# hv of six batches as seven half-size products over even and odd tokens, in a linear-attention and gated-MLP kernel

## The chip, the cores and the metric

The kernel runs on one NeuronCore of one Trainium2 chip. The metric is the device time of one execution in microseconds (us). Before the change it is 513.96 us, the median of two runs (513.74 and 514.18).

## The reference

Eight batches of 576 tokens go through two layers. The attention part has 8 heads of 64 and no softmax: k and v of a head make one 64x64 matrix, q is multiplied by it, and each head's 64 outputs are normalized by their root mean square. The result is `x`, 576 x 512 for a batch. The second part is a spatially gated MLP:

```
kv = einsum('bhsd,bhse->bhde', k, v);  out = einsum('bhsd,bhde->bhse', q, kv)
x  = out / sqrt(mean(out*out) + 1e-6) * g_norm          # heads side by side: 576 x 512
h  = maximum(x @ w_in, 0);  u, v = h[..., :512], h[..., 512:]
v_n = (v - mean(v)) / sqrt(var(v) + 1e-6)
v_s = einsum('ts,bsd->btd', w_spatial, v_n) + b_spatial[None, :, None]
y  = (u * v_s) @ w_out
```

So there are four large products in a batch. In the kernel's names they are hv (x by the V half of w_in), u (x by the U half), the spatial product (w_spatial by v_n) and out (gated by w_out).

## The kernel before, in words

**Number format.** Every large product is made of three TensorE matmuls in place of one. Both operands are split into a high part (a rounding copy on ScalarE, `split`, L325) and a low part (the difference, on VectorE, L326). `hl` lists the three pairs high-high, high-low and low-high. Names that end in H and L are these two parts: XH and XL of x, VH and VL of v_n, GH and GL of the gated product, WVH and WVL of w_in's V half, WUH and WUL of its U half, WSH and WSL of w_spatial.

**Tiles.** 576 tokens are four chunks of 128 and a tail of 64. The tails of two batches, an even and the odd one after it, are computed together in one 128-token chunk (`hv_tail`, and the out unit with the number NC). S is 576, NT 512, HS 288 (half the tokens), HF 256 (half of 512 features).

**The four products of a batch from 2 on.** hv (`hv`, L312) takes the four chunks one by one: 4 steps over the 512 rows of w_in, three pairs each, so 12 matmuls whose moving operand is 512 columns wide. The chunk's x is the stationary operand. `hv_end` then takes it out of PSUM with one ReLU on ScalarE, normalizes it and splits it. u and the spatial product are already made by Winograd's form of Strassen's scheme: seven half-size products p1 to p7 in place of eight (`u_steps` L481, `sp_steps` L574), each for two halves q of 128 rows. A product is 6 matmuls of 288 columns here. It needs sums of quarter blocks of both operands: those of x are made in each batch (`x_sums`, tiles T, L427), those of the V quarter blocks too (`sums`, L343), those of the weights once. p6, p7 and p4 add up in one PSUM bank (b), p5 and p3 in another (c), p1 and p2 in a third (a), and VectorE or ScalarE reads a bank between them. out (`out_unit`, L632) is 12 matmuls of 512 columns for each chunk.

**Buffers.** Four PSUM banks (`ps_mm`) serve all large products. SBUF is full, so two buffers take turns. One holds G (the gated product) during the spatial and out products and the sums T during u. The other holds w_out during out and three extra forms of w_in's U half (UX) during u. Both are refilled from DRAM copies (spare_u, spare_o) by DMAs on GpSimd's queue (`to_u` L861, `to_out` L871).

**Order.** The first two batches are issued from a table of tokens (PLAN, L35), since weights are decoded there from 64-bit numbers. From batch 2 on the loops at L916 to L976 issue, for batch b: `to_u`, `x_sums`, the hv chunks, the seven u products twice, the spatial products, the out chunks. Between them `step()` issues one piece of the attention of a later batch (k-v products `pskv`, q products `pso`, transposes `pstr`, normalizing). Within the limits of data and buffers a list scheduler then settles the order on each engine.

Attention loads go on SyncE's queue, the loads of UX and w_out on GpSimd's.

Of the kernel before, what the change touches and what calls it, by code (L numbers as in the profile page):

```python
# [47 lines left out]
def body(ctx: ExitStack, tc, qT, kvm, kvt, g2, w_in, wsT, bsp, w_out, out):  # L48
# [16 lines left out]
    WVH = persistent([P, NP, FH], F32R, "WVH")  # L65
    WVL = persistent([P, NP, FH], F32R, "WVL")
# [3 lines left out]
    spare_u = dram.tile([P, 2, 2, 3, HF], F32, name="spare_u", tag="spare_u")  # L70
# [5 lines left out]
    WSH = persistent([P, 2, 7, HS], F32R, "WSH")  # L76
    WSL = persistent([P, 2, 7, HS], F32R, "WSL")
# [21 lines left out]
    gcol = persistent([P, 16], F32, "gcol")[:, 0:1]  # L99
    edge = ctx.enter_context(tc.tile_pool(name="edge", bufs=1, side="right"))  # L100
# [216 lines left out]

    def hv_k(c, k, ps):
        cols = slice(c * P, (c + 1) * P)
        pairs = hl(XH[:, k, cols], XL[:, k, cols], WVH[:, k], WVL[:, k])  # L320
        for i, (lt, rh) in enumerate(pairs):
            nc.tensor.matmul(ps, lt, rh, start=k == 0 and i == 0, stop=k == NP - 1 and i == 2)  # L322
# [34 lines left out]
    def hv_tail():  # L357
# [3 lines left out]
                   hl(XH[:, k, cols], XL[:, k, cols], WVH[:, k], WVL[:, k])])  # L361
        v = work.tile([P, FH], F32, name="v", tag="v", bufs=3)
        layer_norm(ps, v, nc.vector)
        d = work.tile([P, HS], F32, name="d", tag="g")[:, 0:HF]
# [10 lines left out]
    def hv_32(c, k):  # L375
        nc.tensor.matmul(psv[c], X32[:, k, c * P:(c + 1) * P], W32[k], start=k == 0,
                         stop=k == NP - 1)

    def hv_tail_32():
# [7 lines left out]
        d = work.tile([P, HS], F32, name="d", tag="g")[:, 0:HF]  # L387
# [25 lines left out]
    def split_g():  # L413
        for d in range(4):
            split(GH[:, d], GL[:, d], U[:, d, 0:NT])
            split(GT[:, 0, d, 0:TAIL], GT[:, 1, d, 0:TAIL], U[:, d, NT:S])

    def u_unit(b, d, j):
# [5 lines left out]
                               XH[:, k, cols], XL[:, k, cols])])  # L424
# [7 lines left out]
    def x_sums_():  # L432
        for k in range(2):
            q = []
            for of, j, name in ((0, 0, "p1"), (2, 1, "u2"), (0, 1, "u3"), (2, 0, "g")):
                q.append(work.tile([P, HS], F32, name=name, tag=name))
                x = [f32(x[:, of + k, j * HS:(j + 1) * HS]) for x in (XH, XL)]
                nc.vector.tensor_tensor(q[-1], *x, op=ALU.add)
            q11, q22, q12, q21 = q
            nc.vector.tensor_tensor(q11, q12, q11, op=ALU.subtract)  # L440
            nc.vector.tensor_tensor(q12, q22, q12, op=ALU.subtract)
            nc.vector.tensor_tensor(q22, q22, q11, op=ALU.subtract)
            nc.vector.tensor_tensor(q21, q21, q22, op=ALU.subtract)
            for n, x in (1, q22), (0, q11), (2, q12), (3, q21):
                split(TH[n][:, k], TL[:, n, k], x)

    def w_sums(kk):
# [8 lines left out]
        for x, n in (first[:, HF:FH], slice(0, 1)), (second, slice(1, 3)):  # L456
# [3 lines left out]
            for i, w in enumerate(parts):  # L460
                nc.sync.dma_start(spare_u[:, i, kk, n], f32(w))

    def u_product(ps, q, n, of, start=True, stop=True):

        cols = slice(q * P, (q + 1) * P)
        raw = {0: (0, 0), 1: (2, 0), 2: (2, 1)}
        pairs = []
        for k in range(2):
            if n < 4:
                w = [x[:, k, n, cols] for x in (WUH, WUL)]  # L470
            else:
                w = [UX[:, i, k, n - 4, cols] for i in range(2)]
            if of in raw:
                at, j = raw[of]
                x = [x[:, at + k, j * HS:(j + 1) * HS] for x in (XH, XL)]
            else:
                x = [TH[of - 3][:, k], TL[:, of - 3, k]]
            pairs += hl(*w, *x)
        multiply(ps, pairs, start, stop)

    def u_steps():  # L481

        st = {}

        def bank(q, name):
            st[q, name] = ps_mm.tile([P, 512], F32, name=f"psu{name}", tag="mm")[:, 0:HS]
            return st[q, name]

        def temp(q, name):
            st[q, name] = work.tile([P, HS], F32, name=name, tag=name)  # L490
            return st[q, name]

        def own(q, i, j):
            return U[:, 2 * i + q, j * HS:(j + 1) * HS]

        def p1(q):
            ps = bank(q, "a")
            u_product(ps, q, 0, 0)
            nc.scalar.copy(temp(q, "p1"), ps)

        def p2(q):
            ps = st.pop((q, "a"))
            u_product(ps, q, 1, 1, False)
            nc.scalar.copy(own(q, 0, 0), ps)

        def p6(q):
            ps = bank(q, "b")
            u_product(ps, q, 3, 4)
            nc.vector.tensor_tensor(temp(q, "u2"), ps, st[q, "p1"], op=ALU.add)

        def p5(q):
            ps = bank(q, "c")
            u_product(ps, q, 6, 3)

        def p7(q):
            ps = st[q, "b"]
            u_product(ps, q, 4, 5, False)
            nc.vector.tensor_tensor(temp(q, "u3"), ps, st[q, "p1"], op=ALU.add)
            nc.vector.tensor_tensor(own(q, 1, 1), st[q, "c"], st.pop((q, "u3")), op=ALU.add)

        def p4(q):
            ps = st.pop((q, "b"))
            u_product(ps, q, 2, 6, False)
            nc.vector.tensor_tensor(own(q, 1, 0), ps, st.pop((q, "p1")), op=ALU.add)

        def p3(q):
            ps = st.pop((q, "c"))
            u_product(ps, q, 5, 2, False)
            nc.vector.tensor_tensor(own(q, 0, 1), ps, st.pop((q, "u2")), op=ALU.add)

        return [lambda f=f, q=q: f(q) for f, q in
                ((p1, 0), (p1, 1), (p2, 0), (p2, 1), (p6, 0), (p5, 0), (p7, 0), (p6, 1), (p4, 0), (p3, 0),
                 (p5, 1), (p7, 1), (p4, 1), (p3, 1))]

    def product(ps, q, n, of, start=True, stop=True):
# [4 lines left out]
                                                      WSH[:, k, of], WSL[:, k, of])], start, stop)  # L540
# [16 lines left out]
    def gate(b, d, j, ps, add=None):  # L557
# [3 lines left out]
        g = work.tile([P, HS], F32, name="g", tag="g")  # L561
# [4 lines left out]
        if j == 0:  # L566
            split(GH[:, d, cols], GL[:, d, cols], g)
# [453 lines left out]
```

## Time and profile before

| | |
|---|---|
| median of the runs shown | 513.96 us |
| the profiled execution | 512.66 us |
| its span, first to last instruction | 510.9 us |
| TensorE busy | 498.2 us (98%) |
| TensorE weight loads busy | 437.9 us (86%) |
| VectorE busy | 412.3 us (81%) |
| ScalarE busy | 291.0 us (57%) |
| GpSimd busy | 21.5 us (4%) |
| moved by DMA | 72.24 MB, 141 GB/s on average |
| mean granted TensorE clock | 0.996 |

The profiled execution takes 1.76 us more than its span, and the median is 1.30 us above it. "PE" is TensorE's matmuls, "PEld" its weight loads, which overlap the matmuls. A matmul's duration in the profile includes the depth of the array, so consecutive matmuls overlap in it; what one costs in a stream is the step from start to start, which is read from a run of matmuls and their count. DVE is VectorE, ACT ScalarE, POOL GpSimd, SP SyncE. Busy shares of TensorE near 100% therefore do not say that no wait is left, while a chain of waits that runs through TensorE's matmuls says that nothing else held it up at that place.

### The profile page before, as it was taken

The page shows a single profiled execution, that of the slowest core. Times are in us where ns is not written, and L with a number is a line of the kernel's source. Part 1 is how long each engine was busy: PE and PEld are TensorE (multiplying, and loading weights), DVE is VectorE, ACT ScalarE, POOL GpSimd, SP SyncE. Part 2 cuts the span into 40 slices and gives each one's busy share as a digit, 9 for nine tenths or more (in the row PEclk, how much of TensorE's full clock was granted, in tenths as well). Part 3 has the DMA queues.
Part 4 walks back from the last instruction along what each step waited for, and adds up shares of the span by engine and source line. Part 5 has one row for each costly group of instructions (what it writes and reads, how often), then busy time and mean ns, then how long its engine had stood idle before and what let it go on. Part 6 is the DMA issues. An engine that isn't in the chain of part 4 may idle for free.

```text
span 510.9 us, 9902 instructions
## 1 busy us (share of the span) xinstructions
PE 498.2 (98%) x3436; PEld 437.9 (86%) x3436; DVE 412.3 (81%) x1266; ACT 291.0 (57%) x1006; POOL 21.5 (4%) x47
## 2 busy tenths in 40 slices
PE   6899999999999999999999999999999999999996
PEld 6648778898988899988998899988998889988995
DVE  3898499789998599968897679977899579997860
ACT  2555455796733697457722688447643578527422
POOL 5000000000000001000000001000000001000000
PEclk8999999999999999999999999999999999999999
DMA  7995400536346616334265614424354511314223
GB/s 253 305 333 197 123 24 1 193 101 207 114 145 216 187 41 212 117 99 181 86 218 189 192 42 139 159 97 165 116 185 141 164 36 49 150 42 164 67 101 103
DMA packets 28071, 72.24 MB, mean 141 GB/s; under 512 B 3506, under 2 KB 8626, under 8 KB 26484
## 3 DMA queue, kind: packets, MB, share of 16 engines
q1 hardware_dynamic: 24564, 49.58, 30.0%
q0 software_dynamic: 3456, 22.02, 12.5%
q8 instruction: 27, 0.44, 0.4%
q14 instruction: 24, 0.20, 0.1%
HBM read 58.48 MB, written 13.11 MB: 140 GB/s over the span
## 4 chain that ended last, share of the span: by engine, by line
PE 72%; DVE 11%; ACT 7%; DMA 7%; SPq 1%; issue 1%; ACTq 0%; DVEq 0%
PE pso L289 18%; PE psh L322 12%; PE psb L544 4%; PE psub L544 4%; PE psc L544 4%; PE pskv L134 4%; PE psua L544 3%; DMA KV<-kvm 3%; PE psu L400 3%; PE pso L209 3%; PE psa L409 2%; PE psa L544 2%; PE psuc L544 2%; PE pstr L237 2%; PE psu L289 2%; DMA qt<-qT 2%
## 5 line engine op out<-in xcount | busy, mean ns | idle before, releaser
L289 PE MATMUL pso<-WO,G 128*128 128x512 f32 x384 | 97.2, 396 | 0.0
L289 PEld LDWEIGHTS pso<-WO,G 128*128 128x128 f32 x384 | 70.3, 188 | 14.1
L325 ACT CAST G<-g 128x288 fp32r<-128x288 f32 (+1 forms) x56 | 22.8, 408 | 61.2 <-DVE g L565 60.8
L192 ACT ACTIVATE x<-pso 128x64 f32<-128x64 f32 x200 | 42.8, 254 | 5.6 <-PE pso L209 5.5
L322 PE MATMUL psh<-WVL,XH 128*128 128x512 f32 x112 | 43.7, 390 | 0.0
L322 PE MATMUL psh<-WVH,XH 128*128 128x512 f32 x112 | 43.5, 393 | 0.0
L322 PE MATMUL psh<-WVH,XL 128*128 128x512 f32 x112 | 43.4, 392 | 0.0
L192 ACT ACTIVATION_READ_ACCUMULATOR x<-pso 128x1 f32 x200 | 42.0, 239 | 0.0
L326 DVE TENSOR_TENSOR VL<-v,VH 128x512 fp32r<-128x512 f32 (+1 forms) x56 | 34.2, 619 | 7.8 <-ACT VH L325 7.6
L646 ACT COPY o<-pso 128x512 f32<-128x512 f32 x35 | 20.3, 593 | 26.0 <-PE pso L289 23.3
L325 ACT CAST VH<-v 128x512 fp32r<-128x512 f32 (+1 forms) x56 | 31.1, 574 | 4.2 <-DVE v L354 3.8
L301 DVE BATCH_NORM_STATS2 s<-v 128x6 f32<-128x512 f32 x32 | 21.8, 690 | 7.3 <-ACT v L295 7.1
L544 PE MATMUL psb<-WSH,VH 128*128 128x288 f32 x84 | 25.4, 304 | 0.3
L295 ACT ACTIVATE v<-psh 128x512 f32<-128x512 f32 x32 | 18.8, 596 | 11.3 <-PE psh L322 7.6
L309 ACT ACTIVATE v<-v,mv,rv 128x512 f32<-128x512 f32 x28 | 23.3, 837 | 3.1 <-DVE mv L308 3.1
L322 PEld LDWEIGHTS psh<-WVH,XH 128*128 128x128 f32 x112 | 21.0, 188 | 4.6 <-ACT o L646 0.2
L322 PEld LDWEIGHTS psh<-WVL,XH 128*128 128x128 f32 x112 | 21.0, 188 | 4.6
L134 PEld LDWEIGHTS pskv<-KV 128*64 128x64 f32 x512 | 17.8, 137 | 8.4 <-issue 4.0
L322 PEld LDWEIGHTS psh<-WVH,XL 128*128 128x128 f32 x112 | 21.0, 188 | 4.4
L544 PE MATMUL psb<-WSL,VH 128*128 128x288 f32 x84 | 24.6, 295 | 0.0
L134 PE MATMUL pskv<-KV 128*64 128x64 f32 x512 | 20.8, 226 | 3.5 <-DMA KV<-kvm 3.5
L326 DVE TENSOR_TENSOR G<-g,G 128x288 fp32r<-128x288 f32 (+1 forms) x56 | 23.3, 417 | 1.1 <-ACT G L325 0.4
(243 smaller groups left out, 1430.1 us busy)
## 6 DMA issues: line engine op xcount, KB each, us to landing
KV<-kvm SPq DMA_DIRECT2D x31, 512.0 KB, 4.7
WO<-spare_o POOLq DMA_DIRECT2D x12, 1024.0 KB, 6.3
UX<-spare_u POOLq DMA_DIRECT2D x12, 768.0 KB, 6.0
out<-o SPq DMA_DIRECT2D x32, 256.0 KB, 2.2
qt<-qT SPq DMA_DIRECT2D x16, 288.0 KB, 4.0
stage<-w_in SPq DMA_DIRECT2D x8, 512.0 KB, 7.0
qt<-qT SPq DMA_DIRECT2D x16, 256.0 KB, 2.9
KT<-kvt SPq DMA_DIRECT2D x32, 64.0 KB, 4.8
```

The lines of the kernel that those rows point to most:

```text
L134: return nc.tensor.matmul(ps[h:h + D, at:at + D], of[:, 0, h:h + D], of[:, 1, h:h + D], start=c == 0, stop=c == NC)
L192: nc.scalar.activation(x[:, cols], ps[0:rows, cols], AF.Square, accum_out=ss[:, h:h + 1])
L209: nc.tensor.matmul(ps[:, c * P:(c + 1) * P], qt[:, c * P:(c + 1) * P], st[p], start=True, stop=True)
L289: nc.tensor.matmul(ps, lt, rh, start=i == 0, stop=i == n - 1)
L295: nc.scalar.activation(v, ps, AF.Relu)
L301: nc.vector.bn_stats(s6, v)
L309: nc.scalar.activation(v, v, AF.Identity, bias=m, scale=r)
L322: nc.tensor.matmul(ps, lt, rh, start=k == 0 and i == 0, stop=k == NP - 1 and i == 2)
L325: nc.scalar.copy(hi, x)
L326: nc.vector.tensor_tensor(lo, x, f32(hi), op=ALU.subtract)
L544: nc.tensor.matmul(ps, lt, rh, start=start and i == 0, stop=stop and i == len(pairs) - 1, skip_group_check=True)
L646: nc.scalar.copy(o, ps)
```

## The change

The hv product of batches 2 to 7 is made by the same scheme of seven products as u. Tokens are divided in even and odd ones, so that 512 tokens are two times 256 and the sums of x (T) that u needs serve hv as well. All places that divided tokens at 288 now divide them by parity: x is read with a stride of two elements as TensorE's moving operand (u) and as its stationary operand (hv), G is written with that stride, and w_spatial and b_spatial arrive from the host with rows and columns in the order even, odd.

One function `seven` issues the products for u and hv. For hv a product is 6 matmuls of 256 columns, and one half q goes through PSUM banks a, b and c as in u. The four-chunk ReLU on ScalarE gives way to copies, adds on VectorE and ReLUs over SBUF. `norm_two` normalizes two tiles at a time.

Four extra forms of w_in's V half (WVX) are made once (`v_sums`, tokens Y0 and Y1) and written to DRAM (spare_v). Four of the seven forms of w_spatial (WSX) are written to DRAM too (spare_s). WVX and WSX take turns in one SBUF buffer: `to_v` loads WVX after the last spatial product of a batch, `to_s` loads WSX after the last hv product. All writes of spare copies move from SyncE's queue to GpSimd's. `move_tail`'s copy of XL moves from GpSimd to ScalarE. The sums of x and the temporaries of the products get tiles of their own (SUM), and x_sums handles both k in one instruction.

The order is now in tables: PLAN is rewritten in places, SEVEN and GATED give the order of the products, FIRST, EVEN and ODD the order of all pieces of a batch (s is a step of attention, v an hv product, u a u product, p a spatial product, o an out chunk, w the sums of w_in's U half, y the tails).

```
+SEVEN = """
...
+p10 p60 p11 p50 p70 p20 p61 p30 p51 p40 p21 p71 p41 p31
...
+GATED = """
...
+p10 p11 p60 p50 p70 p20 p61 p21 p40 p51 p30 p71 p31 p41
...
+EVEN = """
...
+s v s v v v v v v v v v s v v v s v u u s s s s u u y u u u u u u u u s u s u p p p s s p s p p s p
+s s s s p p p p s p s p p s o o o o s s s s
...
+def halves_of(ap, j):
+    return ap.rearrange("p (i j) -> p j i", j=2)[:, j]
...
-    WSH = persistent([P, 2, 7, HS], F32R, "WSH")
+    WSH = persistent([P, 2, 3, HS], F32R, "WSH")
...
+    WSX = pool_s.tile([P, 4, 2, 2, HS], F32R, name="WSX", tag="WSX")
+    NEAR, FAR = {0: 0, 3: 1, 4: 2}, {1: 0, 5: 1, 6: 2, 2: 3}
...
-        nc.gpsimd.tensor_copy(XL[:, :, to], f32(XL[:, :, of]))
+        nc.scalar.copy(XL[:, :, to], f32(XL[:, :, of]))
...
     def x_sums_():
-        for k in range(2):
-            q = []
-            for of, j, name in ((0, 0, "p1"), (2, 1, "u2"), (0, 1, "u3"), (2, 0, "g")):
-                q.append(work.tile([P, HS], F32, name=name, tag=name))
-                x = [f32(x[:, of + k, j * HS:(j + 1) * HS]) for x in (XH, XL)]
+        for k, j, name in ((0, 0, "p1"), (2, 1, "u2"), (0, 1, "u3"), (2, 0, "g")):
+            q.append(SUM[name])
+            x = [f32(x[:, k:k + 2, 0:S]).rearrange("p k (i j) -> p j k i", j=2)[:, j] for x in (XH, XL)]
...
-                nc.sync.dma_start(spare_u[:, i, kk, n], f32(w))
+                nc.gpsimd.dma_start(spare_u[:, n, i, kk], f32(w))
...
+    def v_product(ps, q, n, of, start=True, stop=True):
+        pairs = []
+        for k in range(2):
+            w = [x[:, k, n] for x in (WVH, WVL)] if n < 3 else [WVX[:, n - 3, i, k] for i in range(2)]
+            pairs += hl(*[x[:, q * P:(q + 1) * P] for x in x_form(of, k)], *w)
+        multiply(ps, pairs, start, stop)
...
+    def seven(product, name, cols, own, done):
...
+        def p1(q):
+            ps = new(q, "a")
+            product(ps, q, 0, 0)
+            nc.scalar.copy(own(q, 1, 0), ps)
+        def p2(q):
+            ps = bank.pop((q, "a"))
+            product(ps, q, 1, 1, False)
+            nc.scalar.activation(own(q, 0, 0), ps, AF.Relu)
+        def p6(q):
+            ps = new(q, "b")
+            product(ps, q, 3, 4)
+            nc.vector.tensor_tensor(own(q, 0, 1), ps, own(q, 1, 0), op=ALU.add)
...
+        def p4(q):
+            ps = bank.pop((q, "b"))
+            product(ps, q, 2, 6, False)
+            nc.vector.tensor_tensor(own(q, 1, 0), ps, own(q, 1, 0), op=ALU.add)
+            done(q, 0)
+        def p3(q):
+            ps = bank.pop((q, "c"))
+            product(ps, q, 5, 2, False)
+            nc.vector.tensor_tensor(own(q, 0, 1), ps, own(q, 0, 1), op=ALU.add)
+            done(q, 1)
...
+        def done(q, j):
+            v = tiles[q, j]
+            if j == 0:
+                nc.scalar.activation(v[:, HF:FH], v[:, HF:FH], AF.Relu)
             else:
+                nc.scalar.activation(v, v, AF.Relu)
+                norm_two(q, tiles[q, 0], v)
...
-            nc.sync.dma_start(spare_o[:, i, k], f32(WO[:, i, k]))
+            nc.gpsimd.dma_start(spare_o[:, i, k], f32(WO[:, i, k]))
...
+    def to_v():
+        nonlocal WVX
+        WVX = pool_s.tile([P, 4, 2, 2, HF], F32R, name="WVX", tag="WSX")
+        for n in (0, 3, 1, 2):
+            nc.gpsimd.dma_start(WVX[:, n], spare_v[:, n])
+
+    def to_s():
+        nonlocal WSX
+        WSX = pool_s.tile([P, 4, 2, 2, HS], F32R, name="WSX", tag="WSX")
+        for n in range(4):
+            nc.gpsimd.dma_start(WSX[:, n], spare_s[:, n])
```

**TensorE, between batches 2 and 3.** pso is an out chunk, psh and psha are hv's banks. Before, rows where hv of batch 3 stands inside batch 2's out chunks:

```order
L322 MATMUL psh<-WVH,XH 128x512
L322 MATMUL psh<-WVL,XH 128x512
L289 MATMUL pso_2643<-WO,G 128x512 x2
L289 MATMUL pso_2659<-WO,G 128x512 x2
L322 MATMUL psh<-WVH,XL 128x512
```

Now, directly behind the last of the four out chunks (pso at L258 is attention, T the sums of x):

```order
L662 MATMUL psha<-WVH,XH 128x256
L662 MATMUL psha<-WVL,XH 128x256
L662 MATMUL psha<-WVH,XL 128x256
L258 MATMUL pso<-KVB,qt 128x128 x4
L662 MATMUL pshb<-WVX,T 128x256 x2
```

hv no longer stands among the out chunks, and its second product, which reads T and WVX, comes after one product of 6 matmuls and one step of attention.

**VectorE, in hv and u of batch 3.** v is a tile of hv's output (v_2770 and v_2779 here belong to one half q), VL its low part, U the output of u. Before, a chunk's sums behind its normalizing:

```order
L352 TENSOR_TENSOR v_3622<-v_3589,v_3622 128x256
L179 SCALAR_TENSOR_TENSOR qv_3671<-sv_3670,rv_3672 128x1
L353 TENSOR_TENSOR v_3589<-v_3589 128x256
L180 SCALAR_TENSOR_TENSOR rv_3672<-qv_3671,rv_3672 128x1
L354 TENSOR_TENSOR v_3589<-v_3622,v_3589 128x256
L308 SCALAR_TENSOR_TENSOR mv_3666<-mv_3666,rv_3672 128x1
L355 TENSOR_TENSOR v_3622<-v_3622,v_3589 128x256
L326 TENSOR_TENSOR VL_1007<-v_3589,VH_1006 128x512
```

Now, at the end of that stretch:

```order
L377 TENSOR_TENSOR VL_1072<-v_2770,VH_1071 128x512
L684 SCALAR_TENSOR_TENSOR SUMg_119<-U_106,psa_3145 128x288
L280 SCALAR_TENSOR_TENSOR XL_96<-pstr_3376,gcol_115,XH_95 128x512
L280 SCALAR_TENSOR_TENSOR XL_96<-pstt_3383,gcol_115,XH_95 128x4x64
L377 TENSOR_TENSOR VL_1072<-v_2779,VH_1071 128x512
L405 TENSOR_TENSOR v_2788<-v_2819,v_2788 128x256
L599 TENSOR_TENSOR v_2770<-pshb_2772,v_2770 128x256
```

The read of bank pshb_2772 for product p4 of half 0 (L599) stands behind the sums and splits of the same tile, because p30 precedes p40 in SEVEN and `done` of p3 issues the normalizing.

**GpSimd, from the last fills of the start to batch 2.** Before, MEMSETs, a copy in the tail and the loads of UX and w_out:

```order
masks.py:199 AFFINE_SELECT ident<-ident 128x128
L753 MEMSET TB_98 1x512 x2
L753 MEMSET TB_99 1x512 x2
L869 DMA UX<-spare_u 128x1536 x2
L261 CAST XL<-XL 128x4x64
L875 DMA WO<-spare_o 128x2048 x2
```

Now, from the writes of w_out's copies in batch 1 on:

```order
L837 DMA spare_o<-WO 128x512 x8
L518 DMA spare_u<-w 128x256 x2
L518 DMA spare_u<-w 128x2x256 x2
L986 DMA WVX<-spare_v 128x1024 x4
...
L980 DMA UX<-spare_u 128x1024 x3
L992 DMA WSX<-spare_s 128x1152 x4
L998 DMA WO<-spare_o 128x2048 x2
```

The writes of spare copies stand on this queue, and the load of WVX for batch 2 stands between the two halves of the writes of spare_u (the "..." here stands for the second half, rows like the first). Each later batch issues four kinds of load where it issued two: 4 of WVX, 3 of UX, 4 of WSX and 2 of w_out, against 2 of UX and 2 of w_out before.

More of the change, by code (lines that the diff above doesn't have):

```diff
@@ L460, in w_sums, with v_sums @@
             for i, w in enumerate(parts):
-                nc.sync.dma_start(spare_u[:, i, kk, n], f32(w))
+                nc.gpsimd.dma_start(spare_u[:, n, i, kk], f32(w))
+    def v_sums(kk):
+        first, second = W32[kk], W32[2 + kk]
+        a11, a21, a12, a22 = first[:, 0:HF], first[:, HF:FH], second[:, 0:HF], second[:, HF:FH]
+        x, y = (work.tile([P, FH], F32, name="v", tag="v", bufs=3) for _ in range(2))
+        s2, s3, s4, s1 = x[:, 0:HF], x[:, HF:FH], y[:, 0:HF], y[:, HF:FH]
+        nc.vector.tensor_tensor(s1, a21, a22, op=ALU.add)
+        nc.vector.tensor_tensor(s3, a11, a21, op=ALU.subtract)
+        nc.vector.tensor_tensor(s2, s1, a11, op=ALU.subtract)
+        nc.vector.tensor_tensor(s4, a12, s2, op=ALU.subtract)
+        for n, of in (0, x), (2, y):
+            parts = [w[:, n + kk, 0:FH] for w in (XH, XL)]
+            split(*parts, of)
+            for i, w in enumerate(parts):
+                nc.gpsimd.dma_start(spare_v[:, n:n + 2, i, kk], f32(w).rearrange("p (n f) -> p n f", f=HF))
@@ L479, in u_product @@
[L479 to L533, printed above, removed]
@@ new lines, in norm_two @@
+    def norm_two(q, first, second):
+        mv = small.tile([P, 2, 2], F32, name="mw", tag="mw")
+        for n, v in enumerate((first, second)):
+            s6 = small.tile([P, 6], F32, name="s6", tag="s6")
+            nc.vector.bn_stats(s6, v)
+            nc.vector.bn_aggr(mv[:, n], s6)
+        r = rsqrt(mv[:, :, 1], 2, P, 1.0, "w")
+        m = mv[:, :, 1]
+        nc.vector.scalar_tensor_tensor(m, mv[:, :, 0], -1.0, r, op0=ALU.mult, op1=ALU.mult)
+        for n, v in enumerate((first, second)):
+            nc.scalar.activation(v, v, AF.Identity, bias=m[:, n:n + 1], scale=r[:, n:n + 1])
+        split(VH[:, q, 0], VL[:, q, 0], first[:, 0:HF])
+        split(VH[:, q, 1:3], VL[:, q, 1:3], second.rearrange("p (h f) -> p h f", f=HF))
+        sums(q, first, second)
@@ L560, in gate @@
         cols = slice(j * HS, (j + 1) * HS)
-        g = work.tile([P, HS], F32, name="g", tag="g")
+        g = SUM["g"][:, n_gate[0] % 2]
+        n_gate[0] += 1
         if add is not None:
@@ L914, in body, with first, batch @@
     VH, VL = (vpool.tile([P, 2, 7, HF], F32R, name=f"V{x}", tag=f"V{x}") for x in "HL")
-    def first(b):
+    def first():
+        for c in (0, 2, 1, 3):
+            hv(1, c)
+            step()
+        for d in range(4):
+            if d == 2:
+                enqueue(2)
+                enqueue(3)
+            for j in range(2):
+                u_unit(1, d, j)
+                step()
+            if d < 2:
+                make_out(2 + d)
+                split_out(2 + d)
+                if loads:
+                    loads.pop(0)()
+        nc.gpsimd.dma_start(spare_s[:], f32(WSX[:]))
+    def batch(b):
         if b > 1:
@@ L938, in first @@
-        for n, f in enumerate(u_steps()):
-            if n == 1 and b % 2 == 0:
+            v = v_steps()
+        u, p, o = u_steps(), sp_steps(b), [0, 1] + [NC] * (b % 2) + [2, 3]
+        n_p = n_o = 0
+        if b % 2 and b > 1:
+            enqueue(b + 1)
+            enqueue(b + 2)
+        for token in (FIRST if b == 1 else ODD if b % 2 else EVEN).split():
+            if token == "v":
+                v.pop(0)()
+                if not v:
+                    to_s()
+            elif token == "u":
+                u.pop(0)()
+                if not u:
+                    to_out()
+                    if b % 2 == 0:
+                        enqueue(b + 1, 1)
+            elif token == "p":
+                p.pop(0)()
+                if not p and b < NB - 1:
+                    to_v()
+            elif token == "o":
+                out_unit(b, o.pop(0))
+            elif token == "s":
+                step()
+            elif token == "y":
@@ L965, in body @@
-    first(1)
-    last(0)
-    second(1)
-    last(1)
-    for b in range(2, NB):
-        first(b)
-        if b % 2 == 0:
-            enqueue(b + 1, 1)
-        second(b)
-        last(b)
+            elif token == "w":
+                u_sums(n_p)
+                n_p += 1
         if b % 2 == 0:
             step(len(queue))
+    first()
+    for c in range(NC):
+        out_unit(0, c)
+        step()
+    for b in range(1, NB):
+        batch(b)
 _OUTS = [((B, S, DM), "float32")]
```

212 lines of the change are left out of this document (113 added, 99 removed).

## The prediction, made before the changed kernel ran

> **What bounds the kernel now.** I read the head of the page first, then the chain of waits, a stretch of steady work, the groups of the lines that the change touches, the timeline of VectorE in batch 0, and the DMA queues.
>
> ```profile
> span 510.9 us, 9902 instructions
> PE 498.2 (98%) x3436; PEld 437.9 (86%) x3436; DVE 412.3 (81%) x1266; ACT 291.0 (57%) x1006; POOL 21.5 (4%) x47
> ```
>
> A busy share counts overlapping matmuls as one, so I go on to the chain of waits: its shares, then its rows in order of time (start, duration, engine, tile, line, count) where batch 3 begins, and the busy times of one stretch between two even batches (221 to 339 us, batches 3 and 4).
>
> ```profile
> PE 72%; DVE 11%; ACT 7%; DMA 7%; SPq 1%; issue 1%; ACTq 0%; DVEq 0%
> ...
> 227.08 9.10 PE psh L322 x40
> 236.18 1.58 PE psua L544 x12
> ...
> 242.89 0.89 PE pso L209 x8
> core 0: us, PE busy (x) PEld busy (x) DVE busy (x) ACT busy (x) POOL busy (x), PEclk, DMA share, GB/s
> 221.04:339.30 118.26, 118.20 (x865) 107.74 (x865) 98.18 (x314) 70.24 (x268) 4.63 (x9) 1.00 0.44 144
> ```
>
> The stretch is TensorE's: 118.20 of 118.26 us, at clock 1.00, with VectorE at 98.18 / 118.26 = 83%, near enough to become a second limit. So from batch 2 on time goes where TensorE's columns go, plus any new wait. The three chain rows also give the step of a matmul in a stream: 9.10/40 = 0.2275 us at 512 columns, 1.58/12 = 0.132 at 288, 0.89/8 = 0.111 at 128. The last is far above a quarter of 0.2275, so at 128 columns something other than columns sets the step; the weight load is the candidate (PEld is 107.74 of 118.26 us busy).
>
> **The change part by part.**
>
> *The hv matmuls.* One batch has 4 x 12 = 48 of 512 columns, 48 x 0.2275 = 10.92 us. Now it has 7 products x 2 halves x 6 = 84 of 256. No row has 256 columns. A line through 288 and 512 has slope (0.2275 - 0.1317)/224 = 0.428 ns a column and gives 0.1317 - 32 x 0.000428 = 0.118 us: 84 x 0.118 = 9.91. That is 1.01 us less a batch, 6.0 less in six. Ends: 256 columns as fast as 128 gives 84 x 0.111 = 9.32, a gain of 9.6; 256 no faster than 288 gives 84 x 0.1317 = 11.06, a loss of 0.9. I take the line, since 288 is the near row. In columns it is 84 x 256 = 21504 against 48 x 512 = 24576, an eighth less; what the shorter matmul loses per column takes a quarter of that saving back.
>
> The Trainium skill, "TensorE: Matmul & The Clock Gate", Back-to-back issue gap, puts a 256-column matmul at about 262 cycles, 109 ns warm. By it 84 would cost 9.2 us and the sum would come out some 4.6 us lower. The rows here are slower than that rule at 288 and 512 columns (132 against about 122 ns, 227 against about 216), so I stay with them.
>
> *The seam behind out.* T shares G's buffer, so the casts into T wait for the last out matmul. Before, hv needed no T and stood partly among the out chunks; now product p60, second in order, needs it.
>
> ```profile
> L646 ACT COPY o<-pso 128x512 f32<-128x512 f32 x35 | 20.3, 593 | 26.0 <-PE pso L289 23.3
> L325 ACT CAST T<-u 128x288 fp32r<-128x288 f32 x24 | 10.4, 432 | 1.9 <-PE pso L289 1.9
> L326 DVE TENSOR_TENSOR T<-u,T 128x288 fp32r<-128x288 f32 x24 | 10.9, 453 | 15.8 <-ACT T L325 15.8
> ```
>
> These are groups: line, engine, operation, tiles, count, busy us, mean ns, idle time before them and its cause. One cast now has 576 elements: 0.432 + 288 x (0.593 - 0.432)/224 = 0.64 us. From the last out matmul: its own 0.23, the copy of o that stands ahead on ScalarE 0.59, the cast 0.64, together 1.46 us. TensorE has p10 (6 x 0.118 = 0.71) and one attention piece (4 x 0.111 = 0.44) to do, 1.15. The hole is 0.3 a batch, +1.8 in six. Ends: 0 if the copy goes elsewhere in ScalarE's order; without the cover 1.46 a batch, about +9.
>
> *Taking hv out of PSUM.*
>
> ```profile
> L295 ACT ACTIVATE v<-psh 128x512 f32<-128x512 f32 x32 | 18.8, 596 | 11.3 <-PE psh L322 7.6
> ...
> L353 DVE TENSOR_TENSOR v<-v 128x256 f32<-128x256 f32 x16 | 6.7, 419 | 0.1
> ...
> L326 DVE TENSOR_TENSOR VL<-v,VH 128x512 fp32r<-128x512 f32 (+1 forms) x56 | 34.2, 619 | 7.8 <-ACT VH L325 7.6
> ```
>
> Four ReLUs (L295) a batch go; 10 adds of 256 columns come to VectorE, 10 x 0.42 = 4.2 us by L353. Fewer and larger sums of x give some of it back: 24 instructions a batch of 288 become 12 of 576, at 0.45 against 0.67 us by the L326 rows of 288 and 512 (a column costs (0.619 - 0.453)/224 = 0.74 ns), 10.9 to 8.0. Net +1.3 us a batch, VectorE from 83% to about 85%: hidden, if TensorE does not have to wait for a particular add. One place where it may: `done` of p30 issues the normalizing before p40 of the same tile, so VectorE reads bank b of p40 late, and u starts with three banks free for its products instead of four. The gates of both parities must also be ready before the first out chunk, where before only half the tokens were needed, and hv no longer fills that wait. One late bank costs at most a product, 6 x 0.132 = 0.8 us; I take about a fifth of it a batch, +1 in six, with ends 0 and +4.8.
>
> *v_sums in batch 0.* 8 adds of 256 and 4 splits of 512, 8 x 0.42 + 4 x 0.62 = 5.8 us of VectorE. They stand in the table (Y0, Y1) where VectorE waits:
>
> ```profile
> 48.86 1.00 DVE L305 TENSOR_SCALAR V<-V,mv,rv 128x512 f32<-128x512 f32 x2
> 56.50 0.17 DVE L172 TENSOR_SCALAR ah<-ss 128x8 f32<-128x8 f32 x1 [6.64 <-ACT x L192]
> ```
>
> The timeline's row at 56.50 has 6.64 us of idle before it. I take 0; +5.8 if that hole is gone.
>
> *Spare writes on GpSimd's queue.* In batch 1 the chain runs through output and spare writes on one queue:
>
> ```profile
> 156.69 3.55 DMA out<-o
> 160.75 1.70 DMA spare_u<-w
> 163.17 2.47 DMA spare_u<-w
> 166.93 3.22 DMA out<-o
> ```
>
> The writes of spare_u are 1.70 + 2.47 = 4.2 us of it and now stand elsewhere. TensorE had other work for most of that (the chain follows what ended last, not what stood idle), so I take -1, ends -4.2 and 0.
>
> The Trainium skill, "SBUF — State Buffer", two separate sides, speaks against this move: it says that VectorE's use of the port shared with GpSimd can starve transfers that GpSimd issues. By it WVX and WSX would come late, which is rival D. Here UX, on that queue, lands in 6.0 us (below) with VectorE 83% busy.
>
> *The new loads.*
>
> ```profile
> q1 hardware_dynamic: 24564, 49.58, 30.0%
> q0 software_dynamic: 3456, 22.02, 12.5%
> ...
> WO<-spare_o POOLq DMA_DIRECT2D x12, 1024.0 KB, 6.3
> UX<-spare_u POOLq DMA_DIRECT2D x12, 768.0 KB, 6.0
> ```
>
> The first two are queues (packets, MB, share of the engines' time); the last are issues, with us from issue to landing. WVX is 128 x 4096 x 4 bytes = 2.1 MB, WSX 2.36 MB a batch; with the spare writes about 31 MB are added. q0 needs 0.125 x 510.9 / 22.02 = 2.9 us a MB, so the DMA share in the steady part goes from 0.44 by 8.9 x 2.9 / 118 to about 0.66, WVX takes 6.1 us and WSX 6.8. WVX is issued behind the last spatial product, and the four out chunks (48 x 0.2275 = 10.9 us) and p10 come before its first use; WSX behind the last hv product, with some 14 products of u (14 x 0.79 = 11 us) before its first use. GpSimd's queue carries nothing else that anyone waits for, and its order is the order of use. I take 0.
>
> *Strided reads by TensorE.* No row shows one; on VectorE a read behind `rearrange` is priced like any other in these rows. 0, with the ends in rival C.
>
> Sum: -6.0 + 1.8 + 1 + 0 - 1 = -4.2. The profiled execution of 512.66 becomes 508.5; the median stands 1.30 above it, so **509.8 us**.
>
> **The rivals.**
>
> A, the forecast, 505 to 514: chance 0.54.
>
> B, a larger gain. The step at 256 columns is the 0.111 of 128, the seam is covered and the spare writes' 4.2 come back: -9.6 - 4.2 = -13.8 at most, about 500; half of it on top of the forecast gives 503. For it: PEld is below 100%, so a load might hide. Against: rows at 288 and 512 fit one line. 0.13.
>
> C, slower: TensorE pays for a stride. In hv the x of p1, p2 and p4 is a strided stationary operand (36 matmuls a batch), in u a strided moving one (36): 72 x 6 + 144 in batch 1 = 576. The gain of 4.2 is gone at 7 ns each; slower than before by 2% (10.3 us) needs (10.3 + 4.2) / 576 = 25 ns, a fifth of a step. Half a step more, 63 ns, is +36, about 546. Nothing in the trace speaks for it or against it. 0.08. The Trainium skill, "SBUF — State Buffer", Specifications, tells of reads in lines of 16 bytes, of which a stride of two floats uses half; no run here shows what TensorE makes of that.
>
> D, slower: transfers late. WVX's four pieces land in use order, the last needed by p30, about 10.9 + 7 x 0.71 = 15.9 us after issue. That is 2.6 times 6.1. If loads take 3.1 times as long (VectorE, or 0.66 of share with attention loads), TensorE waits 18.9 - 15.9 = 3 us a batch, +18, about 528. Against: UX's 6.0 us. 0.07.
>
> E, the gain is eaten: one late bank or gate a batch more than I allowed, 1.5 us, +9 in six: 514 to 519. For it: VectorE near 85%, adds of 0.42 us between matmuls of one accumulation, a chain that already spends 11% on VectorE. 0.18.
>
> **How the numbers follow.** The range 502.5 to 519 takes in A, E and most of B; C, D and a part of B, 0.20, lie outside. Below 503.7 (faster by over 2%, which is about what a measurement can tell from no change) lies most of B, 0.10; above 524.2 most of C and D, 0.11; within 2% the rest, 0.79.
>
> **What will show it.** In the changed profile: the step of psha, pshb and pshc over a run of matmuls (0.118; 0.111 is B, over 0.13 ends the gain), separately for strided and plain operands (equal, or C). Idle time of TensorE before pshb behind the last out chunk, ended by ScalarE's cast of T, near 0.3 us; before pshb or psub ended by VectorE, near 0.2. WVX and WSX from issue to landing near 6 to 7 us, nobody waiting on them (else D). No spare_u in the chain of batch 1, and VectorE's work at 50 to 56 us filled without TensorE's start moving. If steady idle of TensorE for two batches is above 4 us, E is right; if the first 220 us move by more than 3 us either way, the sum failed in the place that I priced at -1.

## The result and the profile after

The changed kernel takes **558.31 us** (557.93 to 558.69) against 513.96: 1.086 times, 95% interval 1.082 to 1.091. It is 44.4 us slower. The forecast was 509.8, range 502.5 to 519.

The head of the page after, and its shares of the chain of waits:

```profile
span 556.9 us, 10481 instructions
PE 537.8 (97%) x3652; PEld 469.2 (84%) x3652; DVE 421.1 (76%) x1228; ACT 302.5 (54%) x1067; POOL 64.9 (12%) x123
...
PE 80%; DVE 6%; DMA 6%; ACT 4%; issue 4%; POOL 1%; SPq 0%; ACTq 0%; POOLq 0%; DVEq 0%
```

TensorE has 39.6 us more busy time, while VectorE's share of the span falls (its busy time goes from 412.3 to 421.1). So most of the loss is not new waiting of TensorE: its own work is longer. The chain in order of time shows which (start, duration, engine, tile, line, count), first in batch 1, then in hv and u of batch 3:

```profile
100.81 18.41 PE psu L338 x72
...
251.54 1.41 PE pshb L662 x12
252.95 1.43 PE pshc L662 x12
...
255.52 1.53 PE psua L662 x6
...
260.05 0.80 PE psub L662 x6
260.84 1.55 PE psua L662 x6
```

hv's matmuls of 256 columns step by 1.41/12 = 0.118 us. psub, which reads the sums T, steps by 0.80/6 = 0.133 as before. But psua, which reads x itself with a stride of two, takes 1.53/6 = 0.255, and so do the u units of batch 1, 18.41/72 = 0.256 (row L338). Nothing waits in these rows.

Groups of TensorE instructions of the changed kernel (count, busy us, mean ns, idle time before them), matmuls and weight loads:

```profile
L662 PE MATMUL psua<-XH,WUH 128*128 128x288 f32 x48 | 21.1, 440 | 0.0
...
L662 PE MATMUL psub<-T,WUH 128*128 128x288 f32 x72 | 17.4, 301 | 0.1
...
L662 PE MATMUL pshb<-WVX,T 128*128 128x256 f32 x144 | 22.7, 289 | 1.8 <-DVE v L584 0.6 <-ACT T L376 0.6 <-ACT o L760 0.6
...
L662 PEld LDWEIGHTS pshb<-WVX,T 128*128 128x128 f32 x144 | 19.0, 189 | 2.9 <-ACT T L376 1.0 <-DVE v L584 1.0 <-ACT o L760 0.8
...
L662 PEld LDWEIGHTS psha<-WVH,XH 128*128 128x128 f32 x48 | 9.4, 196 | 1.4 <-ACT v L574 1.2
```

At 256 columns only the operand that moves pays. In psha x is the stationary operand with the same stride: its weight load takes 196 ns in place of 189, but its matmuls step by 1.43/12 = 0.119, where pshb's above step by 0.118 and pshc's by 0.119:

```profile
500.66 1.43 PE psha L662 x12
```

A pair of batches, 3 and 4, by the busy times of a stretch from hv to hv, and the landing times of the loads:

```profile
251.54:378.58 127.04, 126.52 (x939) 115.23 (x938) 99.08 (x294) 71.96 (x271) 13.83 (x26) 1.00 0.61 203
...
WSX<-spare_s POOLq DMA_DIRECT2D x24, 576.0 KB, 5.7
WVX<-spare_v POOLq DMA_DIRECT2D x24, 512.0 KB, 7.0
...
out<-o SPq DMA_DIRECT2D x32, 256.0 KB, 2.1
```

The pair takes 127.04 us against 118.26, 8.8 more. Its 72 strided matmuls at 0.255 - 0.133 = 0.122 us make 8.8. That the two agree so well is in part chance, since hv's shorter matmuls were to save 2.0 in this stretch. In the whole program 36 in each of six batches and 96 in batch 1 make 312, or 38.2 us.

### The profile page after: what moved, and what is told of

Its sections match the earlier page's. It is cut to its first block, busy times and chain, and to the rows that moved or that the text cites. A ratio compares the mean times of both kernels' runs of the same rounds, so it can differ in the third digit from the quotient of the medians.

```text
span 556.9 us, 10481 instructions
## 1 busy us (share of the span) xinstructions
PE 537.8 (97%) x3652; PEld 469.2 (84%) x3652; DVE 421.1 (76%) x1228; ACT 302.5 (54%) x1067; POOL 64.9 (12%) x123
## 4 chain that ended last, share of the span: by engine, by line
PE 80%; DVE 6%; DMA 6%; ACT 4%; issue 4%; POOL 1%; SPq 0%; ACTq 0%; POOLq 0%; DVEq 0%
PE pso L338 13%; PE psua L662 7%; PE psub L662 5%; PE psuc L662 5%; PE pshb L662 5%; PE pso L258 5%; PE psu L338 4%; DMA KV<-kvm 4%; PE pskv L183 3%; PE pshc L662 3%; PE psa L662 3%; PE psu L451 3%; PE psb L662 3%; PE psa L461 3%; PE psha L662 3%
## 5 line engine op out<-in xcount | busy, mean ns | idle before, releaser
L338 PE MATMUL pso<-WO,G 128*128 128x512 f32 x384 | 94.2, 395 | 1.2 <-ACT G L376 0.8
L338 PEld LDWEIGHTS pso<-WO,G 128*128 128x128 f32 x384 | 70.6, 188 | 17.3 <-ACT G L376 2.0
L376 ACT CAST G<-SUMg 128x256 fp32r<-128x256 f32 x56 | 24.1, 431 | 46.7 <-DVE SUMg L684 46.4
L377 DVE TENSOR_TENSOR G<-SUMg,G 128x256 fp32r<-128x256 f32 x56 | 23.4, 417 | 1.8 <-ACT G L376 1.0
L662 PE MATMUL pshb<-WVX,T 128*128 128x256 f32 x144 | 22.7, 289 | 1.8 <-DVE v L584 0.6
L662 PE MATMUL psb<-WSX,VH 128*128 128x288 f32 x112 | 23.9, 304 | 0.0
L279 ACT ACTIVATE XH<-pstr,gcol 128x512 fp32r<-128x512 f32 x28 | 19.2, 693 | 6.8 <-PE psua L662 2.8
L280 DVE SCALAR_TENSOR_TENSOR XL<-pstr,gcol,XH 128x512 fp32r<-128x512 f32 x28 | 20.7, 742 | 2.6 <-ACT XH L279 2.1
L250 DVE TENSOR_TENSOR x<-pso,rh 128x512 f32<-128x512 f32 x32 | 21.9, 686 | 0.9
L662 PEld LDWEIGHTS pshb<-WVX,T 128*128 128x128 f32 x144 | 19.0, 189 | 2.9 <-ACT T L376 1.0
L662 PE MATMUL psua<-XH,WUH 128*128 128x288 f32 x48 | 21.1, 440 | 0.0
L662 PE MATMUL psua<-XH,WUL 128*128 128x288 f32 x48 | 21.1, 440 | 0.0
```

The lines of the kernel that those rows point to most:

```text
L250: nc.vector.tensor_tensor(heads(x), heads(ps[0:rows]), r.unsqueeze(2).broadcast_to([rows, 8, D]), op=ALU.mult)
L279: nc.scalar.activation(hi, ps, AF.Copy, scale=gcol)
L280: nc.vector.scalar_tensor_tensor(lo, ps, gcol, f32(hi), op0=ALU.mult, op1=ALU.subtract)
L338: nc.tensor.matmul(ps, lt, rh, start=i == 0, stop=i == n - 1)
L376: nc.scalar.copy(hi, x)
L377: nc.vector.tensor_tensor(lo, x, f32(hi), op=ALU.subtract)
```

## The experiments

Theory M: the strided moving operand costs about 0.122 us a matmul and makes most of the loss. Rival W: waits (WVX, GpSimd's queue, banks) make it. The kernel before was run again in each of the four sets (512.9 to 514.0), so a difference between runs of different sets is uncertain by about 1 us.

**e1, u's moving operand without the stride.** u then takes other tokens than w_spatial does.

```
-    return [halves_of(x[:, at + k, 0:S], j) for x in (XH, XL)]
+    return [part(x[:, at + k, 0:S], j) for x in (XH, XL)]     # part: plain for u, halves_of for hv
...
-    halves_of(XH[:, k, 0:S], j), halves_of(XL[:, k, 0:S], j))])
+    plain_of(XH[:, k, 0:S], j), plain_of(XL[:, k, 0:S], j))])
```

> The changed kernel, but u's raw x is read as TensorE's moving operand without a stride (columns 0 to 287 and 288 to 575 in place of even and odd ones); hv's stationary operand keeps its stride. The tokens of u then no longer belong to those of w_spatial, so its output is not the reference's. Theory M: a moving operand with a stride of two elements takes about 0.255 us for 288 columns in place of 0.133 (1.53/6 and 0.80/6 in the chain after). 312 matmuls (36 in each of batches 2 to 7, 96 in batch 1) then cost 38 us: the run takes 558.3 - 38 = 520, up to 528 if waits come out that the slow matmuls had covered. Rival W: most of the 44 us are waits for WVX, for spare writes on GpSimd's queue and for PSUM banks; then the run stays above 550.

525.5 us, 1.025 times the kernel before (1.022 to 1.028; 512.9 in this set). The chain where u of batch 3 begins:

```profile
243.22 0.79 PE psua L667 x6
...
246.23 0.79 PE psub L667 x6
247.02 0.79 PE psua L667 x6
```

The two are equal now, and 32.8 of 44.4 us are gone, so M holds. The matmuls alone would give 38; some 5 us come back. 12.6 us remain over the kernel before. The pair of batches that took 127.04 takes 119.3 in e1 (239.24 to 358.51), still about 1 more than the 118.26 before, where hv's shorter matmuls were to save 2.

**e3, that stride alone put into the kernel before.** Here too u then takes other tokens than w_spatial does.

```
-    x = [x[:, at + k, j * HS:(j + 1) * HS] for x in (XH, XL)]
+    x = [strided(x[:, at + k, 0:S], j) for x in (XH, XL)]
...
-    XH[:, k, cols], XL[:, k, cols])])
+    strided(XH[:, k, 0:S], j), strided(XL[:, k, 0:S], j))])
```

> The kernel before with one edit alone: u's raw x is read as the moving operand with a stride of two. Tokens of u are then in another order than those of w_spatial, so its output is not the reference's. Theory M: 312 matmuls at 0.122 us more, 514 + 38 = 552. Rival W: 514, within 2 us.

548.7 us, 1.070 times (1.066 to 1.073), 35.8 us over 512.9. One chain row, 12 matmuls at 0.256 where the kernel before had 1.58 for twelve:

```profile
250.68 3.07 PE psua L548 x12
```

From both sides, then: about 33 taken out, about 36 put in. W falls for the larger part.

**e6, what shape of operand costs what.** The eight u units of batch 1 read x in different shapes, and so other tokens than the reference's.

```
-    halves_of(XH[:, k, 0:S], j), halves_of(XL[:, k, 0:S], j))])
+    *[shaped(x[:, k, 0:S], 2 * d + j) for x in (XH, XL)])])
```

> The changed kernel, where each of the eight u units of batch 1 (12 matmuls of 288 columns) reads x in another shape: plain; runs of 32 with gaps of 32; stride 2 (three units, one of them in two pieces); stride 4 in two pieces; pairs of neighbours with a gap of two; fours with a gap of four. It reads other tokens than the reference's. Theory L (the operand is fetched in pieces of four elements, 16 bytes, and what is not used is lost): 0.133 for plain, runs and fours, 0.255 for stride 2 and pairs, about 0.5 for stride 4, the whole some 1 us shorter than 558.3. Theory S (any step other than one halves the rate): 0.255 for all stride 2 and stride 4, 0.133 for plain, runs, fours and pairs, the whole about 6 us shorter.

556.3 us in a single run. Two successive starts in each unit, from TensorE's timeline (start, modelled duration), in the order plain, runs of 32, stride 2, stride 4, pairs, fours:

```profile
102.16 0.29 PE L360 MATMUL psu<-XH,WUL 128*128 128x288 f32 x1
102.29 0.29 PE L360 MATMUL psu<-XH,WUH 128*128 128x288 f32 x1
...
103.75 0.30 PE L360 MATMUL psu<-XH,WUL 128*128 128x288 f32 x1
103.88 0.30 PE L360 MATMUL psu<-XH,WUH 128*128 128x288 f32 x1
...
107.34 0.44 PE L360 MATMUL psu<-XH,WUH 128*128 128x288 f32 x1
107.60 0.44 PE L360 MATMUL psu<-XL,WUH 128*128 128x288 f32 x1
...
117.35 0.44 PE L360 MATMUL psu<-XH,WUH 128*128 128x288 f32 x1
117.61 0.44 PE L360 MATMUL psu<-XL,WUH 128*128 128x288 f32 x1
...
122.38 0.44 PE L360 MATMUL psu<-XH,WUH 128*128 128x288 f32 x1
122.64 0.44 PE L360 MATMUL psu<-XL,WUH 128*128 128x288 f32 x1
...
124.73 0.30 PE L360 MATMUL psu<-XH,WUH 128*128 128x288 f32 x1
124.86 0.30 PE L360 MATMUL psu<-XL,WUH 128*128 128x288 f32 x1
```

Steps of 0.13, 0.13, 0.26, 0.26, 0.26 and 0.13 us. Neither theory fits: stride 4 is hardly worse than stride 2, 0.261 against 0.256 over a unit (against L), and pairs cost as much as stride 2 (against S). Of the shapes tried, those with four or more neighbours ran at full rate; with one or two of four, the step was twice as long and hardly longer. Three of four was not tried.

**e4 and e10, a division of the tokens in two blocks, stored without a stride.**

```
 def halves_of(ap, j):
-    return ap.rearrange("p (i j) -> p j i", j=2)[:, j]
+    return ap[:, j * (XC // 2):j * (XC // 2) + HS]
...
-    split(halves_of(GH[:, d], j), halves_of(GL[:, d], j), g[:, 0:n])
+    split(GH[:, d, main], GL[:, d, main], g[:, 0:n])
```

> The changed kernel with another division of the tokens: half 0 is tokens 0 to 255 and 512 to 543, half 1 is 256 to 511 and 544 to 575, each stored as one contiguous stretch of 320 columns of XH and XL (288, and 32 for the odd batch's tail). No matmul and no write of G has a stride; the tail product's 128 tokens are copied together on ScalarE, four small copies for two batches. Theory M: as the kernel with the plain moving operand, 520 to 528. Rival W: above 550.

545.8 us, 1.064 times (1.061 to 1.068): 20 us worse than e1, although no step of u is long any more. The landing of outputs, the chain, and a stretch of it (page, chain in order of time, busy times with the clock as the last figure but two):

```profile
out<-o SPq DMA_DIRECT2D x32, 256.0 KB, 4.6
...
289.52 7.54 DMA out<-o
...
298.32 6.38 DMA out<-o
...
305.44 1.65 PE pshc L682 x6
...
300.00:305.00 5.00, 2.82 (x20) 2.27 (x19) 3.14 (x8) 3.02 (x20) 0.00 (x0) 1.00 1.07 376
305.00:312.00 7.00, 6.56 (x43) 6.56 (x44) 3.50 (x13) 5.18 (x27) 0.00 (x0) 0.76 0.25 92
```

With G in two blocks the first out chunks need only half 0 and move ahead of the last spatial product. WVX is issued behind that product, so its 2.1 MB (286.7 to 296.9 us) run beside the first outputs, which land in 7.5 us; the next land in 6.4, beside the load of UX (297.0 to 304.9). Only two buffers hold o, ScalarE waits for one, its PSUM bank stays full, and TensorE stands for 2.06 us. Behind the hole the granted clock is 0.76 for 7 us, so the wait is paid again. It is 0.50 in four stretches of e4 (175.4 to 182.2, 305.2 to 308.5, 366.6 to 373.3 and 434.9 to 441.6 us), each beginning in a hole of TensorE of 2.06 to 3.94 us or at its end, and 1.00 over 20 to 510 us of e1. At half rate these 23.5 us can be at most 12 of the 20. e10 keeps the out chunks behind all spatial products, by order edges on TensorE:

```
+    for p in last_p[-2:]:
+        if ins.engine == mybir.EngineType.PE:
+            tc.add_manual_dep(ins, p.name, ...)
```

> The kernel of e4 (545.8), with all out chunks of a batch kept behind its last spatial product on TensorE. In e4 the first out chunks need only half 0 and stood ahead of the last spatial product; WVX, which is loaded behind that product, then landed among the outputs (out from o took 4.6 us in place of 2.1) and its cover was used up. If that is what separates e4 from e1, it goes to 522 to 528. If it is the tail's copies or their buffers, it stays at 540 or more.

535.5 us, 1.045 times (1.040 to 1.049). That order was worth 10 of the 20 us, no more, so the expectation is missed on the high side. Some 4 of the other 10 lie at the start: u of batch 1 begins at 105.8 us where e1 has 102.1, behind a hole of 1.7 us and a stretch at clock 0.50 (74.7 to 81.4).

**e7, no loads of WVX and WSX** (from e1; hv then multiplies by what is in the buffer).

```
-    WVX = pool_s.tile([P, 4, 2, 2, HF], F32R, name="WVX", tag="WSX")
-    for n in (0, 3, 1, 2):
-        nc.gpsimd.dma_start(WVX[:, n], spare_v[:, n])
+    WVX = WSX[:, :, :, :, 0:HF]
```

> The kernel of e1 (u's moving operand without a stride, 525.5) without the loads of WVX and WSX: both products read what w_spatial's forms left in the buffer, so hv is computed with wrong weights. If late or crowding transfers are the rest of the loss (12.6 us over the kernel before in the same set), it goes to about 516; by the waits of TensorE in e1 just ahead of hv's products (some 3 us) 522; if neither matters, 525.

522.8 us, 1.020 times (1.017 to 1.022). The loads cost 2.7 us of e1, not nothing and not the rest.

**e8, p40 before p30** (from e1).

```
-p10 p60 p11 p50 p70 p20 p61 p30 p51 p40 p21 p71 p41 p31
+p10 p60 p11 p50 p70 p20 p61 p40 p51 p30 p21 p71 p41 p31
```

> The kernel of e1 with p40 issued before p30 in the table SEVEN, so that bank b of half 0 is read before the tile is normalized. By the term for banks in the prediction (1 us, at most 4.8): 524.5, not under 520. If the bank is the rest of the loss: about 515. If nothing waits for it: 525.

534.6 us, 1.040 times (1.037 to 1.044): 9 us slower than e1, against all three expectations. In the changed kernel the tile of half 0 is normalized without p40's share: p40 is added behind it and used by nothing, so that kernel, and every version here that makes hv by seven products except e8, leaves a part of hv out. In e8 the tile is normalized with it and must wait for it. One group of spatial products then waits longer:

```profile
L667 PE MATMUL psa<-WSX,VH 128*128 128x288 f32 x56 | 11.7, 307 | 2.7 <-ACT SUMp L712 2.7
```

In e1 the same group has 0.7 us of idle time before it. That is 2 us of 9; where the other 7 go was not settled. Since the swap brings this new wait, it does not test the bank alone. What speaks against a late bank b as the rest of the loss is e1's own trace: TensorE's idle time before pshb that VectorE ends is 0.6 us in all.

**e9, spare writes on SyncE's queue as before** (from e1).

```
-    nc.gpsimd.dma_start(spare_u[:, n, i, kk], f32(w))
+    nc.sync.dma_start(spare_u[:, n, i, kk], f32(w))     # and spare_v, spare_o, spare_s
```

> The kernel of e1 with all writes of spare copies on SyncE's queue, as before the change. By the prediction (1 us gained by the move) 526.5. Rival: the writes on GpSimd's queue hold up the load of WVX for batch 2 (12 us of queue time lie in the chain there, and TensorE waits about 2.6 us at 162 to 183 us): 522.

527.5 us, 1.029 times (1.025 to 1.034). Beside e1's 1.022 to 1.028 the two can't be told apart; the rival's 522 is excluded.

**e16, hv as four plain chunks in all batches** (from e1, without the loads).

```
-    v = v_steps()
+    v = [lambda c=c: hv(b, c) for c in (0, 2, 1, 3)] + [lambda: None] * 10
```

> e1 (moving operand without a stride, 525.5), but hv of all batches as four plain chunks and no load of WVX and WSX. What is left over the kernel before is the new order and the work for the extra forms. e14 stood 10 us under e11 by the same edit. If hv as seven products costs 10 net here too: 515 or 516, close to the kernel before. If the 2.7 us of reloads are all that it loses and the matmuls' 6 us count: 529. If the new order is what costs the 12.6 us: 523 to 527.

524.5 us, 1.021 times (1.019 to 1.022). So hv as seven products, loads and all, costs about as much as it saves (525.5 against 524.5); without its loads it would save 1.8 (522.8, e7), which is near what sets differ by. And 11 us of loss are there without it. Busy times from hv of batch 1 to the end, of the kernel before, then of e16 and of e1 (three kernels, one fence each):

```profile
86.00:510.90 424.90, 419.15 (x2951) 379.01 (x2950) 347.00 (x1081) 249.87 (x887) 14.26 (x27) 1.00 0.40 133
```

```profile
85.00:522.70 437.70, 426.44 (x2952) 381.37 (x2950) 346.49 (x1046) 253.91 (x902) 26.09 (x47) 1.00 0.41 134
```

```profile
85.00:523.30 438.30, 421.86 (x3170) 386.66 (x3168) 351.62 (x1036) 255.53 (x915) 51.72 (x95) 1.00 0.58 195
```

TensorE stands idle 5.8 us before, 11.3 in e16 and 16.4 in e1; in e16 it is also 7.3 us longer busy over the same matmuls (e14 below accounts for some 2 of these). In the stretches that end where u of batches 2, 4 and 6 begins, and in the rest, e16 takes 5.5, 0.5, 2.7 and 4.1 us more than the kernel before; a part of the first is attention that moved ahead (657 matmuls in place of 640). So the loss is spread, with more in batch 1 and at the end than between. Which row of the tables makes which was not settled.

**e11, e12, e14, e15: even and odd tokens stored apart**, so that all operands are read without a stride and G stays as in the changed kernel.

```
-    split_x(ps, XH[:, p, 0:NT], XL[:, p, 0:NT])
+    split_x(ps.rearrange("p (i j) -> p j i", j=2), main_of(XH[:, p]), main_of(XL[:, p]))
```

> The changed kernel with even and odd tokens stored apart: ScalarE and VectorE write them to two stretches of XH and XL (320 columns each, as in e4) when they take the transposes out of PSUM, and all matmuls then read them without a stride, moving and stationary. G and the out chunks stay as in the changed kernel. The tail's 128 tokens are copied together on ScalarE for each two batches. If the strided moving operand is the whole difference between the changed kernel and e1: 525 to 528, as e1. If the copies or their buffers cost what e4 and e10 lost beyond e1: 535 or more.

548.1 us, 1.065 times (1.063 to 1.068). The strided operand is gone and the time is not e1's. e12 makes hv of batches 6 and 7 from plain chunks, e14 of all batches:

```
+    v = v_steps() if b in (2, 3, 4, 5) else [plain chunks]      # e14: in none
```

> e11, but hv of batches 6 and 7 as four plain chunks, as before, with no load of WVX and WSX for them. In the trace of e1 TensorE waits some 6 us in the last two batches, where no attention is left to stand between products. If these waits come from hv as seven products behind out, e12 is 3 to 5 us under e11 (6 saved, 2 of the gain given up); if not, 1 to 2 us over it.

> e11, but hv of all batches as four plain chunks, as before: what is left of the change is the new tables, the tokens' order, the writes of spare copies and the work for the extra forms (which are made and written, never loaded). By the prediction's terms (6.0 gained by matmuls, 1.8 and 1 lost at the seam and the banks, 2.7 lost to reloads by e7) it stays within 1 us of e11. If waits eat more than the matmuls save, it is 3 to 10 us under e11, near 515 to 520; if hv as seven products nets a gain, it is 3 us or more above.

e12: 544.6 us, 1.059 (1.055 to 1.063). e14: 537.9 us, 1.046 (1.044 to 1.048). e12 stands 3.5 under e11, as expected for waits in the last two batches, but e14 stands 10 under it, a like amount for every two batches, so the last two are nothing special; the level of 515 to 520 is missed. In this layout hv as seven products costs 10 us net, where e1 and e16 differ by 1.

e14 also prices the stationary operand's stride at 512 columns. One batch's hv as four chunks, in e16, where x is stationary with a stride of two, and in e14, where it has none (one chain row each):

```profile
231.69 11.20 PE psh L378 x48
```

```profile
245.51 10.90 PE psh L391 x48
```

The step is 11.20/48 = 0.233 against 10.90/48 = 0.227 us, the latter as in the kernel before. 336 such matmuls make some 2 us of e16's loss, and without them hv as seven products would lose about 3 us against e16, not 1.

e14's rows show a loss at the start (groups by form; a piece of TensorE's timeline; busy times with clock):

```profile
L295 ACT ACTIVATE XH<-pstt,gcol 128x128 fp32r<-128x128 f32 x14 | 5.1, 366 | 8.9 <-PE pstt L312 3.5 <-DVE XL L296 3.5 <-DMA spare_v<-XH 1.9
...
L296 DVE SCALAR_TENSOR_TENSOR XL<-pstt,gcol,XH 128x128 fp32r<-128x128 f32 x14 | 4.8, 345 | 14.2 <-ACT XH L295 10.5 <-DMA spare_v<-XL 3.7
...
73.49 1.38 PE L274 MATMUL pso<-KVO,qt 128*128 128x128 f32 x8 [1.94 <-DVE XL L296]
...
66.00:94.00 28.00, 25.03 (x96) 18.90 (x95) 25.10 (x69) 12.96 (x31) 0.00 (x0) 0.82 0.04 11
```

The tail of batch 1 overwrites columns of XH and XL that v_sums uses as scratch and that are still being copied to DRAM. e15 moves the scratch in e11:

```
-    parts = [w[:, n + kk, 0:FH] for w in (XH, XL)]
+    parts = [main_of(w[:, n + kk]) for w in (XH, XL)]
```

> e11 (548.1), with one edit: v_sums puts its temporaries into columns of XH and XL where no tail lies. In e11 the tail of batch 1 is written over columns whose copy to DRAM still runs, and ScalarE and VectorE wait (1.9 and 3.7 us in e14, ended by the DMA of spare_v), with TensorE idle 2.2 and 1.3 us at 73 to 76 us and its clock at 0.7 to 0.8 behind. If that is the start's part of the loss: 538 to 543, and the first spatial products of batch 1 stand 4 to 6 us earlier. If not: 546 to 550.

540.2 us, 1.052 (1.048 to 1.056), as expected. The waits on the DMA are gone and the clock holds:

```profile
L296 DVE SCALAR_TENSOR_TENSOR XL<-pstt,gcol,XH 128x128 fp32r<-128x128 f32 x14 | 4.8, 346 | 4.8 <-ACT XH L295 4.7
...
66.00:94.00 28.00, 26.97 (x126) 21.52 (x124) 26.75 (x72) 15.54 (x35) 2.21 (x4) 1.00 0.12 43
```

Waits of 1.9 and 3.7 us on two engines' queues, with the slower clock behind them, were worth 8 us of run. What keeps e15 15 us above e1 was not settled. No version here beats the kernel before.

## Why the prediction was wrong

The failing step is "Strided reads by TensorE ... 0": it was the largest term, +38 by the rows, +33 and +36 by e1 and e3. The argument for 0 came from other engines' rows (VectorE), and no row of TensorE was there to bound it. The rest of the sum would have failed without it too: e1, which has no strided moving operand, still takes 525.5, above the range's 519. The two ends for an operation that the trace does not show should have come from TensorE's own full rate and half of it: 0 and 312 x 0.13 = 41 us. Rival C had the mechanism and its 25 ns threshold, but spread it over 576 matmuls, stationary and moving, at half a step; it is a full step on the 312 that move. Its chance of 0.08 kept it out of the range.

Of the other steps:

- **hv's matmuls, 0.118 us at 256 columns:** right (1.41/12). The Trainium skill's 109 ns ("TensorE: Matmul & The Clock Gate", Back-to-back issue gap) is 9 ns below it; by that figure the six batches would have come to some 4.5 us less, not the 4.6 of the prediction.
- **The seam behind out, +1.8:** the group pshb<-WVX,T has 1.8 us of idle before it, of which 1.2 by T's cast and the copy of o, as argued, and 0.6 by VectorE. That the total meets the forecast is in part luck.
- **VectorE:** 99.08 us for two batches, against 98.18 + 2.6 = 100.8 forecast. Right.
- **v_sums in batch 0, 0:** right. hv of batch 1 begins at 84.4 us, before at 86.3.
- **Banks, +1:** the 0.6 us by VectorE just named is all that the trace after shows of it. Swapping p40 and p30 cost 9 (e8), but there the normalizing also waits for p40, so it says little on the bank.
- **Spare writes, -1:** too small to be told (e9). Its sign in the profile failed: the chain after still has a write of spare_u, 3.40 us at 177.62, just ahead of hv's pshb products of batch 2.
- **Loads, 0:** pieces land in 5.7 and 7.0 us, but taking them away saves 2.7 (e7), and where the out chunks move ahead of them they collide with outputs (e4). "GpSimd's queue carries nothing else that anyone waits for" overlooked SyncE's outputs: in the changed kernel these land in 2.1 us behind the loads, in e4 in 7.5 beside one.
- **What the sum left out:** the new order, about 11 us (e16, some 2 of them the stationary operand's stride at 512 columns). The prediction read the order of pieces only where hv stands and gave the rest nothing.

The sentence on the Trainium skill, "SBUF — State Buffer", Specifications, would not have helped: it asks for at least two hits in a line of 16 bytes for full bandwidth, and stride 2 and pairs both have two and run at half (0.26 us). Here the measurement decides.

The price rests on two opposite edits that agree within 3 us. The 11 us of the order is a difference of two kernels, not an explanation.

## What to carry to other kernels

Before a layout is chosen for its algebra, ask of every matmul which operand moves and whether its columns are neighbours: here the strided moving operand cost a full second step (0.255 for 0.133 us), the strided stationary one about 6 ns a matmul at 512 columns (e16 against e14) and no step that shows at 256. Where a trace shows no such operation, take the bound from that engine's own rates and weigh it by how many instructions carry it. In an order tuned by hand, a change that frees one product to start earlier, or reuses a scratch region, can cost more than the matmuls it saves.

## What was not expected of the hardware

- TensorE's moving operand ran at full rate (0.133 us for 288 columns) when read in fours with gaps or runs of 32, and at half with one or two of four neighbours, stride 4 (0.261) hardly slower than stride 2 (0.256; e6).
- After a hole of 2.06 us in the middle of thin work the granted clock was 0.76 over the next 7 us (e4), and it was 0.82 over 28 us at the start of e14, with holes of 1.94 and 1.03 us, against 1.00 in e15 without the longer one. The Trainium skill, "TensorE: Matmul & The Clock Gate", Part 1, tells of an idle window of some 3.4 us after which the clock halves; the three holes of this item, as TensorE's rows show them, were each shorter (of e4's other three one was longer, 3.94 us).
- A load of 2.1 MB beside outputs of 256 KB made these take 7.5 us from issue to landing (e4), in place of a median of 2.1.
